# A ring for x, three key-feature buffers and a new opening order in a fused attention and rational-function kernel

## The chip, the cores and the metric

The kernel runs on one core of a Trainium2 chip. The metric is the time of one execution on the device in microseconds (us), as the median of several runs. Beside it stands one profiled execution, with every instruction of each engine: PE (TensorE matmuls), PEld (its weight loads), DVE (VectorE), ACT (ScalarE), POOL (GpSimd) and SP (SyncE, which here only issues DMAs).

## What is computed

There are 4 batches, 4 heads, 1088 positions and head dimension 32; the sketches have 8 rows, the second part has d_model = 128 and d_ff = 2048, on 4 x 1088 = 4352 tokens.

```python
def phi(x):                                    # 8 x 8 = 64 features of each row
    a = einsum('rd,bhsd->bhsr', S1, x); b = einsum('rd,bhsd->bhsr', S2, x)
    return einsum('bhsi,bhsj->bhsij', a, b).reshape(*x.shape[:-1], 64)
q_p, k_p = phi(q), phi(k)
kv = einsum('bhsf,bhsd->bhfd', k_p, v); z = k_p.sum(axis=2)
attn = einsum('bhsf,bhfd->bhsd', q_p, kv) / (einsum('bhsf,bhf->bhs', q_p, z)[..., None] + 1e-6)
x = attn.transpose(0, 2, 1, 3).reshape(4352, 128)
h = x @ w_in
g = (a[0] + a[1]*h + a[2]*h*h + a[3]*h*h*h) / (1 + abs(b[0])*abs(h) + abs(b[1])*h*h + 1e-6)
out = g @ w_out
```

## The kernel before

**Two halves, one list.** The attention half makes x, transposed (feature by token), in the tile xT; the second half reads xT and writes the output. All of it is written as small steps, and the list ORDER at the top of the file says in which sequence they are emitted, as `name:index`. Each engine runs its own instructions in that sequence and waits for others only through data, so a step's place in the list fixes its place in the queue of every engine that it uses, SP's queue of DMAs too.

**Keys.** For each batch, `kt` transposes the keys on DVE, `ks` makes the two sketches on PE, `kc` copies the second sketch out of PSUM on ACT, `kf` multiplies the sketches into the 64 features on DVE (tile k_p), `kp` multiplies the features with v on PE, and `kk` copies the result (kvz) on ACT. The first batch is cut into three parts (2, 2 and 5 of the nine 128-row tiles) and four transposes, kt0 to kt3; its keys come in three DMAs, the columns of the first four tiles as one and the rest as two. Sketches of the first batch lie in the two large PSUM buffers (`wide`, tile h_ps), later ones in the four small banks (`bank`, tile att_ps); both kinds are handed out in turn. k_p has two buffers.

**Queries.** Each batch is cut into blocks, numbered through, 4 in the first batch and 3 in the others. `qt` transposes (DVE), `qs` sketches (PE), `qc` copies (ACT; from block 3 on through DRAM, with DMAs on SP), `qf` multiplies (DVE), `qp` multiplies with kvz (PE), `qd`, `qi`, `qx` divide (ACT or DVE, then DVE), `qb` transposes back (PE) and `qk` copies the block into xT (ACT).

**The second half** works on 17 units of up to 4096 columns (unit 0: 256 tokens; then 512 tokens each in two units; at the end two of 256 tokens). `h` is the hidden matmul of a quarter of the unit (PE, tile h_ps), `e` its copy to bf16 (ACT, tile hh), `u`, `w`, `y` build the denominator on DVE, `ln` and `ex` invert it on ACT (tile r), `pa` or `pd` is one polynomial term on ACT or DVE (tile p, chosen by P_ON_ACT), `s`, `m`, `x` multiply on DVE, `G` is the output matmul (PE) and `st` transposes the output (DVE) and stores it (SP). In `u0`, `s1` and so on the digit is the half of the unit.

**Opening.** `tn` emits idle matmuls, as many as TURNS says at that index, on a bank of their own; a turn with 0 only takes a bank. `lw`, `lx`, `lk`, `lq`, `lv` issue loads of w_out, w_in, keys, queries and v. `wo` scales one of six half-parts of w_out to bf16, on ACT where W_ENG is 1, else on DVE; indices 2y and 2y+1 are the halves for factor y. The single v buffer, the single key buffer and the single kT make their next loads and transposes wait for their last readers.

The lines that a sentence can't say:

```python
self.take = wide if first else bank                                   # Keys
k_p = self.k_p[part] = tmp.tile([128, 5, H, R, R], FP, name="k_p")    # pool of two
nc.scalar.copy(out=xT[:, c:c + self.n], in_=self.xp[:, :self.n])      # Queries.keep
rhs=xT[:, t0:t0 + tl]                                                 # hidden
```

Of the kernel before, what the change touches and what calls it, by code (L numbers as in the profile page):

```python
# [25 lines left out]
ks0:1 y0:0 h1:1 lk:2 kc1:1 ex1:0 lq:2 kf1:1 h3:1 e1:1 s1:0 kc0:1 h0:1 e3:1 kf0:1 pa0:0 m1:0 h2:1 qf:3 e0:1 x1:0 qp:3
qc:4 e2:1 kt0:2 h0:2 ln0:0 u1:1 kt1:2 h1:2 w1:1 e0:2 ex0:0 y1:1 ks0:2 h2:2 e1:2 s0:0 qd:3 ln0:1 h3:2 qi:3 m0:0 e2:2
lk:3 qx:3 kp1:1 x0:0 e3:2 ex0:1 u1:2 qb:3 lv:2 G0:0 pd0:1 qk:3 w1:2 ln1:1 G1:0 G2:0 qf:4 G3:0 kc0:2 kk:1 y1:2 ex1:1
G4:0 G5:0 kf0:2 qp:4 ln0:2 s0:1 qs:5 G0:1 qd:4 qc:5 qi:4 ex0:2 qt:7 G1:1 qx:4 m0:1 qb:4 ks1:2 qk:4 s1:1 pa1:1 h2:3
s0:2 kc1:2 m1:1 h3:3 e2:3 kf1:2 h1:3 e3:3 st:0 x1:1 ln1:2 qs:7 x0:1 h0:3 e1:3 kt1:3 m0:2 h2:4 e0:3 pd1:2 pa0:2 u1:3  # L30
h3:4 qt:9 w1:3 e2:4 G2:1 ex1:2 x0:2 h0:4 qf:5 e3:4 kp1:2 s1:2 pa0:3 y1:3 h1:4 qc:7 e0:4 m1:2 ln0:3 qp:5 kt0:3 e1:4
G3:1 x1:2 ex0:3 G4:1 m0:3 G5:1 u1:4 ks0:3 qd:5 ln1:3 qi:5 G0:2 w1:4 G1:2 pa1:3 qx:5 G2:2 y1:4 lv:3 qb:5 G3:2 qk:5
ex1:3 h0:5 m1:3 v0:3 kk:2 ln0:4 h2:5 s1:3 e0:5 qs:6 G4:2 qf:7 ex0:4 h1:5 x0:3 qt:8 qc:6 e2:5 s0:4 e1:5 h3:5 pd0:4
pa1:4 m0:4 h1:6 v1:3 e3:5 x0:4 G5:2 ln1:4 u1:5 h3:6 st:2 e1:6 w1:5 qp:7 ex1:4 x1:3 h0:6 e3:6 y1:5 qd:7 pa0:5 lq:3 G0:3
G2:3 qi:7 s1:4 h2:6 e0:6 m0:5 ln0:5 m1:4 qs:8 G3:3 e2:6 qf:6 G5:3 x1:4 ex0:5 G0:4 u1:6 G1:4 qc:8 ln1:5 qp:6 v0:5 qx:7
w1:6 qb:7 qd:6 G2:4 pa0:6 qi:6 G3:4 qx:6 y1:6 qb:6 qk:7 G4:4 qk:6 ex1:5 h3:7 m0:6 pa1:5 G5:4 qt:10 s1:5 h1:7 e3:7 st:4
h2:7 e1:7 m1:5 ln0:6 x0:5 h0:7 e2:7 x1:5 qs:9 e0:7 h3:8 qf:8 ex0:6 u1:7 h1:8 v0:6 qc:9 ln1:6 w1:7 ks1:3 s0:6 e1:8 G0:5
y1:7 kc1:3 qp:8 ex1:6 h2:8 pd1:6 kc0:3 e3:8 s1:6 ln0:7 h0:8 kf0:3 e2:8 m1:6 G2:5 ex0:7 G3:5 x0:6 G4:5 kf1:3 qd:8 e0:8
qs:10 G5:5 ln1:7 qi:8 u1:8 kp1:3 qx:8 pa0:7 w1:8 qb:8 G0:6 qf:9 qk:8 y1:8 qc:10 h3:9 ex1:7 s0:7 h2:9 e3:9 s1:7 ln0:8
h0:9 m0:7 e2:9 x1:6 G2:6 e0:9 h1:10 x0:7 ex0:8 pd1:7 h1:9 m1:7 pa0:8 s0:8 G3:6 e1:9 u1:9 G0:7 qt:11 ln1:8 qp:9 qt:12  # L40
# [29 lines left out]
def kernel(  # L70
# [161 lines left out]
    class Keys:  # L232
        def __init__(self, b, k_sb, v_sb, first=False):
            self.b, self.dst, self.k_sb, self.v_sb = b, kvz[b % 2], k_sb, v_sb
            self.take = wide if first else bank
# [16 lines left out]

        def sketches(self, part):
            t0, n = self.PARTS[part]
            ab = self.ab[part] = self.take()[:, 0:n * H * 2 * R].rearrange("p (t h s r) -> p t h s r", h=H, s=2, r=R)
            for t in range(t0, t0 + n):
                nc.tensor.matmul(ab[:, t - t0].rearrange("p h s r -> p (h s r)"),  # L257
                                 lhsT=self.kT[:, t * 128:(t + 1) * 128],
                                 rhs=S12.rearrange("p h s r -> p (h s r)"), start=True, stop=True)
# [5 lines left out]

        def features(self, part):
            n = self.PARTS[part][1]
            k_p = self.k_p[part] = tmp.tile([128, 5, H, R, R], FP, name="k_p")
            nc.vector.tensor_mul(
                out=k_p[:, 0:n].rearrange("p t h i j -> p (t h) i j"),  # L270
                in0=self.ab[part][:, :, :, 0, :].rearrange("p t h r -> p (t h) r")[:, :, :, None]
                    .broadcast_to([128, n * H, R, R]),
                in1=self.sk[part][:, 0:n].rearrange("p t h r -> p (t h) r")[:, :, None, :]
                    .broadcast_to([128, n * H, R, R]))
# [38 lines left out]
    class Queries:  # L313
# [74 lines left out]

        def keep(self):
            c = self.b * S + self.c0  # L390
            nc.scalar.copy(out=xT[:, c:c + self.n], in_=self.xp[:, :self.n])
# [50 lines left out]
    def hidden(i, part):  # L442
# [3 lines left out]
        for x in range(per // 4):  # L446
            f = f0 + part * (per // 4) + x
            nc.tensor.matmul(t[:, x * tl:(x + 1) * tl], lhsT=w_in_sb[:, f * 128:(f + 1) * 128],  # L448
                             rhs=xT[:, t0:t0 + tl], start=True, stop=True)
# [261 lines left out]
```

## Time and profile before

| what | value |
|---|---|
| median of 3 runs | 273.89 us (273.89 to 274.06) |
| the profiled execution | 274.08 us |
| its span, first to last instruction | 272.3 us |
| busy PE / DVE / ACT | 258.4 / 256.0 / 250.2 us |
| DVE busy from 0 to 30.72 us | 20.3 us |
| granted TensorE clock, mean | 0.999 |

A row of the timeline begins with its start and its duration in us, then engine, line, operation, `written tile<-read tiles`, shape and count; in brackets at the end is the idle time before it and what ended it. A duration includes an instruction's way through the pipeline, so the next one can start before it is over. A row of groups ends with the busy time, the mean of one in ns, and the engine's idle time ahead of the group. L12 is line 12 of the kernel.

### The profile page before, as it was taken

How to read it: one execution, taken by the hardware profiler on the slowest of the kernel's cores; microseconds unless marked ns; L12 is line 12 of the kernel's file. 1: busy time of each engine (PE TensorE's matmuls, PEld its weight loads, DVE VectorE, ACT ScalarE, POOL GpSimd, SP SyncE). 2: the span in 40 equal slices, each digit the busy share in tenths (PEclk: the TensorE clock that was granted, in tenths of full speed). 3: DMA queues.
4: the chain of work that ended last, by engine and by line, in shares of the span. 5: the costliest groups of instructions: out<-in, count | busy, mean ns of one | idle time of the engine just before them, and what ended most of it. 6: DMA issues, size and time to landing. Idle time of an engine off the chain costs nothing.

```text
span 272.3 us, 3730 instructions
## 1 busy us (share of the span) xinstructions
PE 258.4 (95%) x1398; PEld 146.2 (54%) x1398; DVE 256.0 (94%) x277; ACT 250.2 (92%) x224; POOL 2.9 (1%) x24
## 2 busy tenths in 40 slices
PE   7989999999999899999999999999999998999763
PEld 2778656963564354545454554434545356675552
DVE  2876999999999999999999999999999999999993
ACT  1467999998999999999999999999999999999990
...
DMA packets 30530, 19.55 MB, mean 72 GB/s; under 512 B 20400, under 2 KB 26672, under 8 KB 30512
## 3 DMA queue, kind: packets, MB, share of 16 engines
...
q10 hardware_dynamic: 1520, 0.38, 0.7%
...
q14 instruction: 7, 0.06, 0.1%
...
## 4 chain that ended last, share of the span: by engine, by line
PE 35%; ACT 28%; DVE 23%; issue 9%; DMA 2%; SPq 1%; DVEq 0%; ACTq 0%
PE h_ps L448 17%; PE att_ps L581 9%; ACT hh L454 8%; ACT ln L539 7%; ACT r L543 7%; DVE s L547 4%; ACT p L534 4%; DVE g L551 4%; PE att_ps L361 3%; DVE g L562 3%; DVE w L488 3%; DVE w L483 2%; DMA k_sb<-in_k_dram 2%; PE att_ps L298 1%; PE att_ps L257 1%
## 5 line engine op out<-in xcount | busy, mean ns | idle before, releaser
L448 PE MATMUL h_ps<-xT,w_in_sb 128*128 128x512 f32 (+1 forms) x320 | 126.2, 536 | 2.3 <-ACT hh L454 1.6
L448 PEld LDWEIGHTS h_ps<-xT,w_in_sb 128*128 128x128 f32 x320 | 58.3, 190 | 52.8 <-issue 35.0
L454 ACT CAST hh<-h_ps 128x1024 bf16<-128x1024 f32 x68 | 68.2, 1022 | 4.2 <-PE h_ps L448 3.7
L581 PEld LDWEIGHTS <-w_out 128*128 128x128 bf16 x460 | 44.6, 98 | 46.0 <-issue 15.1
L543 ACT ACTIVATE r<-ln 128x2048 bf16<-128x2048 f32 (+1 forms) x35 | 65.9, 1883 | 0.3
L539 ACT ACTIVATE ln<-w 128x2048 f32<-128x2048 bf16 (+1 forms) x35 | 65.9, 1882 | 0.3
L534 ACT ACTIVATE p<-hh,a_sb 128x2048 bf16<-128x2048 bf16 (+1 forms) x23 | 46.7, 2035 | 0.1
L547 DVE TENSOR_TENSOR s<-hh,r 128x2048 bf16<-128x2048 bf16 (+2 forms) x33 | 40.9, 1243 | 0.2
L488 DVE TENSOR_TENSOR w<-w,u 128x4096 bf16<-128x4096 bf16 (+2 forms) x22 | 39.5, 1798 | 0.1
L581 PE MATMUL att_ps<-g,w_out 128*128 128x512 bf16 (+1 forms) x160 | 34.8, 347 | 3.6 <-DVE g L562 3.6
L551 DVE TENSOR_TENSOR g<-hh,s 128x2048 bf16<-128x2048 bf16 (+1 forms) x30 | 35.2, 1175 | 0.0
L581 PE MATMUL att_ps<-r,w_out 128*128 128x512 bf16 (+1 forms) x160 | 35.0, 347 | 0.0
L562 DVE TENSOR_TENSOR g<-g,p 128x2048 bf16<-128x2048 bf16 (+1 forms) x30 | 34.9, 1175 | 0.0
L581 PE MATMUL att_ps<-s,w_out 128*128 128x512 bf16 (+1 forms) x140 | 29.8, 343 | 0.9 <-DVE s L547 0.9
L483 DVE TENSOR_SCALAR w<-u,b_abs 128x4096 bf16<-128x4096 bf16 (+2 forms) x22 | 23.9, 1092 | 0.1
L477 DVE TENSOR_SCALAR u<-hh 128x4096 uint16<-128x4096 uint16 (+2 forms) x22 | 21.2, 968 | 0.9 <-ACT hh L454 0.8
L361 PEld LDWEIGHTS att_ps<-kvz,q_pT 128*128 128x128 f32 x144 | 17.6, 191 | 4.9 <-ACT sk_sb L408 1.0
L361 PE MATMUL att_ps<-kvz,q_pT 128*128 128x66 f32 x144 | 18.0, 274 | 0.9 <-DVE q_pT L353 0.5
L298 PEld LDWEIGHTS att_ps<-v_sb,k_p 128*64 128x64 f32 (+1 forms) x288 | 8.8, 138 | 2.6 <-issue 1.8
L529 DVE TENSOR_SCALAR p<-hh,a_sb 128x2048 bf16<-128x2048 bf16 x12 | 9.6, 799 | 0.0
L298 PE MATMUL att_ps<-v_sb,k_p 128*64 128x64 f32 (+1 forms) x288 | 9.5, 224 | 0.0
L425 DVE TENSOR_TENSOR q_pT<-a_all,b_all 128x768 f32<-128x768 f32 (+1 forms) x10 | 9.0, 896 | 0.0
...
## 6 DMA issues: line engine op xcount, KB each, us to landing
...
```

The source lines that it names most:

```text
L361: nc.tensor.matmul(self.nd[:, o:o + 2 * KW], lhsT=self.q_p[:, c, x:x + 128], rhs=kvz[self.b % 2][:, c, :], start=True, stop=True)
L448: nc.tensor.matmul(t[:, x * tl:(x + 1) * tl], lhsT=w_in_sb[:, f * 128:(f + 1) * 128], rhs=xT[:, t0:t0 + tl], start=True, stop=True)
L454: nc.scalar.copy(out=live[i]["hh"][:, part * PW:(part + 1) * PW], in_=live[i]["h", part])
L483: nc.vector.tensor_scalar(out=t[:, c], in0=live[i]["u"][:, c], scalar1=ab1, scalar2=ab0, op0=AX.mult, op1=AX.add)
L488: nc.vector.tensor_mul(out=t[:, c], in0=t[:, c], in1=live[i]["u"][:, c])
L534: nc.scalar.activation(out=part_of(i, "p", h), in_=hh, func=ACT.Identity, scale=a3, bias=a2)
L539: nc.scalar.activation(out=t, in_=live[i]["w"][:, span(h)], func=ACT.Ln, bias=1.0 + 1e-6)
L543: nc.scalar.activation(out=part_of(i, "r", h), in_=live[i]["ln"], func=ACT.Exp, scale=-1.0)
L547: nc.vector.tensor_mul(out=part_of(i, "s", h), in0=hh, in1=part_of(i, "r", h))
L551: nc.vector.tensor_mul(out=part_of(i, "g", h), in0=hh, in1=part_of(i, "p" if horner(i, first(h)) else "s", h))
L562: nc.vector.tensor_mul(out=g, in0=g, in1=part_of(i, "s" if horner(i, first(h)) else "p", h))
L581: nc.tensor.matmul(outs[t0][:, :tl], lhsT=w_sb[y][:, f0 + x, :], rhs=part_of(i, key, h)[:, c:c + tl], start=done[0] == 0, stop=done[0] == ...
```

## The change

Five things are changed.

- k_p gets three buffers in place of two.
- xT holds 2048 tokens and is used as a ring: token t lies at `(t - 256) % 2048`. A block that crosses the ring's edge is copied in two pieces; this is so for one block (tokens 2176 to 2560, cut at 2304).
- Of the first keys' sketches only the third part still lies in a large PSUM buffer; the first two lie in small banks.
- The first keys' loads change queues: the columns of the first four tiles are now issued by ACT, the others of the same rows by SP. The third, small one stays on ACT.
- ORDER is new, with TURNS and W_ENG. The four first transposes run in the order kt0, kt1, kt2, kt3 instead of kt0, kt2, kt3, kt1. All idle matmuls, 12 + 2 + 1 + 2, stand ahead of the first sketch; before, 12 stood there and 2 after the sketches. All three key parts are sketched, multiplied and summed ahead of the second query block; the products of block 2 (`qp:2`) stand ahead of the first hidden matmul, the sketch of block 3 (`qs:3`) behind two or three of them. w_out's part 3 is made on DVE instead of ACT. On SP's queue both halves of w_in precede the second keys, and v precedes the queries. From about the 250th of the 727 steps on, only neighbours are swapped. (LX is read nowhere.)

```diff
-TURNS = (10, 2, 0, 0, 2, 0, 0, 0, 0)
+TURNS = (12, 2, 0, 0, 1, 2, 0, 0, 0)
 ORDER = """
-tn:4 tn:0 lw:1 kt0:0 lq:0 kt2:0 lw:0 kt3:0 lx:1 kt1:0 ks0:0 lk:1 qt:0 ks2:0 kc0:0 lx:0 kf0:0 ba:0 qt:1 tn:1 kc2:0 qs:0
-kf2:0 kp0:0 qc:0 ks1:0 qf:0 kc1:0 kf1:0 qs:1 wo:1 qt:3 kp1:0 qc:1 kp2:0 qf:1 qt:2 qs:3 wo:4 kk:0 lq:1 lv:1 wo:2 qp:0
-wo:0 qs:2 qd:0 wo:5 qi:0 qx:0 qc:2 qb:0 qf:2 qk:0 wo:3 qp:1 kt0:1 qc:3 h2:0 qd:1 qi:1 qx:1 qt:5 h3:0 e2:0 qt:4 kt1:1
+tn:0 lw:1 lq:0 kt0:0 lw:0 kt1:0 lx:1 tn:1 kt2:0 lx:0 tn:4 kt3:0 tn:5 lk:1 ks0:0 qt:0 qt:1 ks1:0 kc0:0 ks2:0 kf0:0
+kc1:0 kf1:0 qs:0 kc2:0 kf2:0 kp0:0 qc:0 kp1:0 ba:0 qf:0 kp2:0 wo:3 qs:1 kk:0 lv:1 qt:3 qp:0 qt:2 qc:1 wo:1 lq:1 qf:1
+qs:2 qd:0 qi:0 qc:2 qp:1 qx:0 qf:2 wo:0 qb:0 qp:2 qd:1 wo:4 qk:0 qi:1 h3:0 qx:1 qd:2 wo:5 wo:2 h2:0 e3:0 kt1:1 kt0:1
...
-W_ENG = (1, 1, 0, 1, 0, 1)
+W_ENG = (1, 1, 0, 0, 0, 1)
...
-    nc.sync.dma_start(out=k0.rearrange("p (m x) -> p m x", m=NM)[:, :, 0:4 * D],
+    nc.scalar.dma_start(out=k0.rearrange("p (m x) -> p m x", m=NM)[:, :, 0:4 * D],
...
-    nc.scalar.dma_start(out=k0[:, 0:km].rearrange("p (m x) -> p m x", m=NM - 1)[:, :, 4 * D:],
+    nc.sync.dma_start(out=k0[:, 0:km].rearrange("p (m x) -> p m x", m=NM - 1)[:, :, 4 * D:],
...
-    xT = big.tile([d_model, n_tok], FP, name="xT")
+    XR = 2048
+    xT = big.tile([d_model, XR], FP, name="xT")
+
+    def x_at(t):
+        return (t - n_tok % 512) % XR
...
-            self.take = wide if first else bank
...
-            ab = self.ab[part] = self.take()[:, 0:n * H * 2 * R].rearrange("p (t h s r) -> p t h s r", h=H, s=2, r=R)
+            ab = (wide if self.first and part == 2 else bank)()[:, 0:n * H * 2 * R]
+            ab = self.ab[part] = ab.rearrange("p (t h s r) -> p t h s r", h=H, s=2, r=R)
...
-            k_p = self.k_p[part] = tmp.tile([128, 5, H, R, R], FP, name="k_p")
+            k_p = self.k_p[part] = tmp.tile([128, 5, H, R, R], FP, name="k_p", bufs=3)
...
-            nc.scalar.copy(out=xT[:, c:c + self.n], in_=self.xp[:, :self.n])
+            cut = min(self.n, XR - x_at(c))
+            for x, y in ((0, cut), (cut, self.n)):
+                if x < y:
+                    nc.scalar.copy(out=xT[:, x_at(c + x):x_at(c + x) + y - x], in_=self.xp[:, x:y])
...
-                             rhs=xT[:, t0:t0 + tl], start=True, stop=True)
+                             rhs=xT[:, x_at(t0):x_at(t0) + tl], start=True, stop=True)
```

More of the change, by code (lines that the diff above doesn't have):

```diff
@@ L26 @@
[L26 to L40, printed above, removed]
@@ new lines @@
+ln1:0 h2:1 w0:0 qt:6 y0:0 kc1:1 ex1:0 h0:1 kf1:1 e2:1 ks0:1 s1:0 e0:1 h1:1 m1:0 kc0:1 pa0:0 kf0:1 h3:1 lq:2 kt0:2 e1:1
+x1:0 e3:1 h0:2 ln0:0 u1:1 h2:2 qf:3 w1:1 qc:4 e0:2 qp:3 e2:2 kt1:2 y1:1 ex0:0 h1:2 s0:0 h3:2 ln1:1 m0:0 kp1:1 e3:2
+x0:0 qd:3 e1:2 qi:3 pd0:1 ex1:1 G0:0 qx:3 lv:2 u1:2 G1:0 ln0:1 G2:0 w1:2 lk:3 G3:0 y1:2 qs:5 kk:1 ex0:1 qb:3 G4:0
+ks0:2 qk:3 qf:4 G5:0 kc0:2 ln0:2 kf0:2 qp:4 s0:1 qc:5 G0:1 qd:4 ex0:2 qi:4 qx:4 G1:1 s1:1 qb:4 ks1:2 qk:4 s0:2 pa1:1
+h2:3 kt1:3 m0:1 kc1:2 h3:3 qt:7 e2:3 m1:1 kf1:2 h0:3 e3:3 ln1:2 x1:1 qs:7 h1:3 x0:1 e0:3 st:0 m0:2 h2:4 e1:3 pd1:2
@@ new lines @@
+pa0:2 h3:4 u1:3 qf:5 e2:4 kp1:2 w1:3 qc:7 ex1:2 x0:2 h0:4 e3:4 s1:2 pa0:3 qt:9 qp:5 y1:3 e0:4 h1:4 qd:5 m1:2 ln0:3
+G2:1 qi:5 x1:2 G3:1 e1:4 kt0:3 lv:3 G4:1 ex0:3 u1:4 ks0:3 G5:1 m0:3 pa1:3 G0:2 w1:4 G1:2 ln1:3 qx:5 G2:2 y1:4 qb:5
+G3:2 qk:5 ex1:3 h0:5 m1:3 kk:2 v0:3 ln0:4 h2:5 s1:3 G4:2 e0:5 ex0:4 qf:7 h1:5 x0:3 e2:5 qs:6 s0:4 qc:6 e1:5 h3:5 pd0:4
+pa1:4 m0:4 h1:6 v1:3 x0:4 e3:5 G5:2 e1:6 u1:5 qp:7 ln1:4 qt:8 st:2 h3:6 w1:5 ex1:4 x1:3 G0:3 e3:6 h0:6 y1:5 pa0:5 lq:3
+G2:3 s1:4 h2:6 e0:6 m0:5 qd:7 ln0:5 G3:3 qi:7 m1:4 G5:3 e2:6 qf:6 qs:8 ex0:5 x1:4 G0:4 G1:4 u1:6 qc:8 ln1:5 qp:6 v0:5
@@ new lines @@
+qx:7 w1:6 qb:7 qd:6 pa0:6 G2:4 qi:6 G3:4 qx:6 y1:6 qb:6 qk:7 G4:4 qk:6 ex1:5 h3:7 m0:6 pa1:5 G5:4 s1:5 h1:7 e3:7 qt:10
+h2:7 st:4 e1:7 m1:5 ln0:6 h0:7 x0:5 e2:7 x1:5 e0:7 h3:8 qf:8 ex0:6 u1:7 qs:9 v0:6 h1:8 qc:9 ln1:6 w1:7 ks1:3 s0:6 e1:8
+G0:5 y1:7 kc1:3 ex1:6 qp:8 h2:8 pd1:6 kc0:3 e3:8 s1:6 ln0:7 h0:8 kf0:3 e2:8 m1:6 G2:5 ex0:7 x0:6 G3:5 G4:5 kf1:3 qd:8
+e0:8 qs:10 G5:5 ln1:7 qi:8 u1:8 kp1:3 qx:8 pa0:7 w1:8 qf:9 qb:8 G0:6 qk:8 y1:8 qc:10 ex1:7 h3:9 s0:7 h2:9 e3:9 s1:7
+ln0:8 h0:9 m0:7 e2:9 x1:6 G2:6 e0:9 h1:10 x0:7 ex0:8 pd1:7 h1:9 m1:7 pa0:8 s0:8 G3:6 e1:9 u1:9 G0:7 qt:11 ln1:8 qp:9
@@ new lines @@
+qt:12 u0:9 m0:8 h3:10 e1:10 w1:9 qd:9 ex1:8 qf:10 h2:10 x0:8 e3:10 x1:7 G4:6 kk:3 e2:10 h0:10 y1:9 pa0:9 w0:9 qp:10
+qi:9 y0:9 e0:10 G1:7 qx:9 qd:10 ln0:9 qi:10 s1:8 qb:9 G5:6 u1:10 G2:7 qk:9 ex0:9 G3:7 qx:10 m1:8 qb:10 G4:7 qk:10
+pd1:8 ln1:9 qs:11 s0:9 h1:11 qc:11 w1:10 ex1:9 h0:11 m0:9 e1:11 x1:8 G5:7 e0:11 h3:11 y1:10 pa1:9 G0:8 s1:9 e3:11
+h2:11 ln0:10 x0:9 h0:12 m1:9 e2:11 pd0:10 ex0:10 h1:12 u1:11 x1:9 G1:8 ln1:10 G2:8 w1:11 G3:8 e0:12 s0:10 G0:9 e1:12
+y1:11 G4:8 ex1:10 G5:8 G1:9 m0:10 ln0:11 G2:9 qf:11 h2:12 s1:10 ex0:11 x0:10 h3:12 pa1:10 m1:10 qs:12 s0:11 G3:9 qc:12
@@ new lines @@
+e2:12 G4:9 pd0:11 ln1:11 G5:9 m0:11 qp:11 x1:10 e3:12 G0:10 x0:11 qd:11 ex1:11 G1:10 qi:11 u1:12 G2:10 pa1:11 qx:11
+G3:10 w1:12 qb:11 G4:10 qk:11 s1:11 pa0:12 h1:13 y1:12 h3:13 e1:13 m1:11 ln0:12 h2:13 st:6 x1:11 ex0:12 G5:10 qf:12
+G0:11 st:10 e3:13 qp:12 s0:12 e2:13 st:8 h0:13 ln1:12 m0:12 u1:13 h2:14 e0:13 x0:12 ex1:12 u0:13 h3:14 w1:13 e2:14
+w0:13 y1:13 e3:14 h1:14 qd:12 pa1:12 y0:13 h0:14 s1:12 e1:14 qi:12 m1:12 G1:11 e0:14 G2:11 qx:12 ln1:13 u1:14 G3:11
+x1:12 qb:12 G4:11 ex1:13 w1:14 G5:11 G0:12 qk:12 pd0:13 ln0:13 h0:15 y1:14 ex0:13 h2:15 pd1:13 s1:13 e0:15 G1:12 s0:13
@@ new lines @@
+ln0:14 G2:12 h3:15 m1:13 e2:15 m0:13 ex0:14 h1:15 x1:13 x0:13 e3:15 G3:12 e1:15 G4:12 s0:14 ln1:14 G0:13 u1:15 G5:12
+m0:14 h2:16 pa0:14 w1:15 h3:16 ex1:14 st:12 y1:15 G1:13 e2:16 e3:16 h1:16 x0:14 ln0:15 u2:16 u3:16 h0:16 w2:16 s1:14
+ex0:15 w3:16 G2:13 y2:16 pd0:15 e1:16 G0:15 y3:16 e0:16 G3:13 s0:15 pa1:14 u0:16 G1:15 m0:15 G4:13 ln1:15 w0:16 G5:13
+m1:14 G0:14 ex1:15 y0:16 G1:14 G2:14 v1:14 ln0:16 G3:14 pd1:15 s1:15 ex0:16 x0:15 x1:14 G2:15 ln2:16 m1:15 G5:14
+ex2:16 s0:16 G0:16 pa0:16 x1:15 G3:15 st:14 ln3:16 m0:16 G4:15 ex3:16 s2:16 G1:16 x0:16 pa2:16 G5:15 m2:16 pa3:16
@@ L57 @@
+G2:16 s3:16 G3:16 x2:16 G4:16 st:15 G5:16 m3:16 G6:16 G7:16 x3:16 G8:16 st:16
 """.split()
-W_ENG = (1, 1, 0, 1, 0, 1)
+W_ENG = (1, 1, 0, 0, 0, 1)
 P_ON_ACT = (1, 1, 0, 1, 1, 0, 1, 1, 0, 1, 1, 1, 1, 0, 1, 0, 1, 0, 1, 1, 0, 1, 0, 1, 1, 1, 0, 0, 1, 1, 0, 0, 1, 1)
@@ L61 @@
 QUARTER = (16,)
-LX = 2
+LX = 4
 TAIL = 2
```

18 lines of the change are left out of this document (1 added, 17 removed).

## The prediction

> **What bounds the kernel now.** I read the busy time in three stretches first, then who waited for whom after the opening, then the opening instruction by instruction. The stretches (columns: span, then busy us and count of PE, weight loads, DVE, ACT, POOL, granted clock, DMA share, GB/s):
>
> ```profile
> 0.00:30.72 30.72, 28.10 (x219) 20.47 (x220) 20.30 (x41) 18.12 (x30) 2.92 (x24) 1.00 0.80 221
> 30.72:264.00 233.28, 226.64 (x1151) 122.90 (x1150) 232.09 (x231) 231.02 (x195) 0.00 (x0) 1.00 0.21 52
> 264.00:272.30 8.30, 3.64 (x32) 2.84 (x30) 3.63 (x7) 1.04 (x1) 0.00 (x0) 0.97 0.43 64
> ```
>
> From 30.72 to 264 us DVE is idle 233.28 - 232.09 = 1.19 us and ACT 2.26 us. Two engines are full there, so the end is fixed by when that stretch begins, by the work in it, and by the few waits left. The waits from 30 to 262 us (total, times, longest) are these:
>
> ```profile
> DVE u L477 <- ACT hh L454: 0.6, 2, 0.3
> ACT hh L454 <- PE h_ps L448: 1.1, 2, 0.7
> ```
>
> In the first 30.72 us DVE is idle 10.42 us. That is the only large store of time, and the new order works there. From roughly the 250th step on, the two orders differ in swaps of neighbours only. So I work out when DVE and ACT reach the same point of their work (the end of the second y of unit 0, at 30.72 us before) and carry that difference to the end.
>
> **The opening on TensorE, step by step.** First the weight loads of two idle matmuls and the start of the twelfth, then TensorE's whole opening (start, duration, what it waited for):
>
> ```profile
> 5.00 0.15 PEld L170 LDWEIGHTS <-idle 128*128 128x128 bf16 x1 [0.28 <-issue]
> 5.43 0.15 PEld L170 LDWEIGHTS <-idle 128*128 128x128 bf16 x1 [0.28 <-issue]
> 5.70 0.38 PE L170 MATMUL att_ps<-idle 128*128 128x512 bf16 x1
> ```
>
> ```profile
> 1.19 4.89 PE L170 MATMUL att_ps<-idle 128*128 128x512 bf16 x12 [1.19 <-DVE idle L165]
> 6.51 2.05 PE L257 MATMUL h_ps<-S,kT 128*128 128x64 f32 x14 [0.43 <-DVE kT L251]
> 8.39 0.59 PE L170 MATMUL att_ps<-idle 128*128 128x512 bf16 x2
> 8.92 1.13 PE L334 MATMUL h_ps<-qT,SAB 64*128 64x256 f32 x8
> 9.98 0.69 PE L298 MATMUL att_ps<-v_sb,k_p 128*64 128x64 f32 x16
> 10.60 0.66 PE L257 MATMUL h_ps<-S,kT 128*128 128x64 f32 x4
> 11.46 1.13 PE L334 MATMUL h_ps<-qT,SAB 64*128 64x256 f32 x8 [0.21 <-DVE q_pT L350]
> 12.53 1.85 PE L298 MATMUL att_ps<-v_sb,k_p 128*64 128x64 f32 x56
> 14.21 0.44 PE L402 MATMUL att_ps<-qT,S 128*64 128x160 f32 x4
> 14.87 1.11 PE L361 MATMUL att_ps<-kvz,q_pT 128*128 128x66 f32 x8 [0.22 <-ACT kvz L308]
> 15.91 1.13 PE L334 MATMUL att_ps<-qT,SAB 64*128 64x256 f32 x8
> 17.02 0.41 PE L387 MATMUL att_ps<-ident,x_tok 128*128 128x128 f32 x2
> 17.96 1.11 PE L361 MATMUL att_ps<-kvz,q_pT 128*128 128x66 f32 x8 [0.52 <-DVE q_pT L353]
> 18.90 0.43 PE L448 MATMUL h_ps<-xT,w_in_sb 128*128 128x256 f32 x1
> ```
>
> *Idle matmuls.* Before, 12 stand ahead of the first sketch and 2 after it; now 12 + 2 + 1 + 2 = 17 stand ahead and none after. The spacing is 5.43 - 5.00 = 0.43 us while the array is slow and 8.39's two take 0.59 - 0.38 = 0.21 us when it is fast; the twelfth starts 0.27 us after its load, so the change falls near 5.6 us. Twelve are issued by 5.91, five more at 0.21 end at 7.0. The first sketch, which waited for kT until 6.51, now waits for them: +0.5.
>
> *Key sketches.* The three parts follow each other on the three transposes, now in the same order as TensorE wants them. Before, 14 passes went from 6.51 to 8.39 with one stop of some 0.2 for a transpose, so 0.12 each; 18 are 2.15: 9.15. Then the first query sketch, 9.98 - 8.92 = 1.06: 10.2, against 9.98 before.
>
> *Key products.* Before, 16 passes at 9.98, a stop for one part's late sketch, then 56 at 12.53. Now all parts are sketched, and 72 passes run through if the features come: 0.62 + (14.21 - 12.53) = 2.3: 12.5. The features of the long part set this:
>
> ```profile
> 8.59 0.29 ACT L264 COPY b_sk<-h_ps 128x160 f32<-128x160 f32 x1 [0.24 <-PE h_ps L257]
> ...
> 8.92 1.49 DVE L269 TENSOR_TENSOR k_p<-h_ps,b_sk 128x1280 f32<-128x1280 f32 x1 [0.17 <-ACT b_sk L264]
> ```
>
> The copy starts 0.2 after the sketches' issue: 9.3 to 9.6; the product runs 9.6 to 11.1. TensorE reaches it after the first two parts at 10.2 + 0.62 + 0.5 = 11.3, so it is covered by 0.2. This is what the third buffer does: with two, this third product would wait until the first part's matmuls ended (10.8), 1.2 us later. The own banks for the first two parts keep the third's sketch from waiting for their features in the same way. The ring itself only makes room; its reads are over a ring's length old, so I give its waits nothing, and its one wrapped copy at most one more 0.39 of ACT (row at 17.61 below).
>
> *Queries.* Second query sketch 12.53 - 11.46 = 1.07: 13.55. Block 0's products 15.91 - 14.87 = 1.04: 14.6. Block 2's sketch 17.02 - 15.91 = 1.11: 15.7. Block 1's products 18.90 - 17.96 = 0.94: 16.65. The transposes back 0.41: 17.05. Block 2's products, which ran after the first hidden matmuls, 0.94: **18.0**, where the first hidden matmul starts, against 18.90. The gaps of 0.22 and 0.52 before 14.87 and 17.96 go because the kv copies and block 1's features are early. That is -0.9 in spite of one block more and five idle matmuls.
>
> *The other feeds.*
>
> ```profile
> 17.07 0.65 ACT L344 COPY a_all<-att_ps 128x256 f32<-128x256 f32 x2
> 17.61 0.39 ACT L391 COPY xT<-att_ps 128x256 f32<-128x256 f32 x1
> 17.87 1.17 ACT L616 ACTIVATE w_out<-w_out_sb_f,a_sb 128x1024 bf16<-128x1024 f32 x1
> ...
> 22.61 1.01 ACT L454 CAST hh<-h_ps 128x1024 bf16<-128x1024 f32 x1 [0.71 <-PE h_ps L448]
> 23.65 2.10 ACT L534 ACTIVATE p<-hh,a_sb 128x2048 bf16<-128x2048 bf16 x1
> ...
> 28.39 1.94 ACT L539 ACTIVATE ln<-w 128x2048 f32<-128x2048 bf16 x1
> ```
>
> The copy at 17.07 follows its sketch by 1.16, so now 15.75 to 16.4; one w_out part (1.17) and x (0.39) follow: x at 18.0, level with TensorE. One w_out part goes from ACT (1.17) to DVE:
>
> ```profile
> L618 DVE TENSOR_SCALAR w_out<-w_out_sb_f,a_sb 128x1024 bf16<-128x1024 f32 x1 | 0.7, 744 | 0.0
> ```
>
> On DVE its 0.74 stands where DVE next waits for the second query sketch (till 13.6), from 11.7 to 12.4, so it is hidden there; uncovered it costs 0.74.
>
> *To the full stretch.* From the hidden matmuls on, the second evacuation keeps its distance of 22.61 - 18.90 = 3.71: 21.7. ACT's p follows 1.04 later, at 22.75. On DVE the second u and y of unit 0 close the opening:
>
> ```profile
> 22.09 1.04 DVE L321 STREAM_TRANSPOSE qT<-q_sb 128x384 f32<-128x384 f32 x2 [2.13 <-DMA q_sb<-in_q_dram]
> ...
> 28.00 0.69 DVE L477 TENSOR_SCALAR u<-hh 128x2048 uint16<-128x2048 uint16 x1
> ...
> 29.58 1.23 DVE L488 TENSOR_TENSOR w<-w,u 128x2048 bf16<-128x2048 bf16 x1
> ```
>
> ACT then has p, a sketch copy, two evacuations and two x copies as before (the last 23.65 to 28.39), so ln starts at 27.5, -0.9. The two x copies end there, so the last evacuation ends at about 26.95, and DVE's second u starts; u, w, one transpose and y take 3.1 (28.00 to 30.72 before, and 0.4 for the transpose): 30.05, **-0.7** against 30.72, with the w_out part already done.
>
> Further on, DVE gets one wait more and loses one:
>
> ```profile
> L547 DVE TENSOR_TENSOR s<-hh,r 128x2048 bf16<-128x2048 bf16 x29 | 35.0, 1212 | 0.2
> ```
>
> Unit 1's u needs its four evacuations: ACT has ln 1.94, r about the same, p 2.10, four evacuations of 1.01 and small copies of 0.6 ahead, less 0.1 of overlap each: 27.5 + 9.8 = 37.3. DVE comes there from 30.05 with two key features (1.49, 1.2), s, m and x (1.21 each) and a transpose (1.07), less overlap: 36.9. The query features, which filled this before, now stand behind. So 0.4 is lost; 0.2 of wait ahead of an s goes, and ACT is 0.2 further ahead than DVE and gives the rest back. -0.7 stands. Of the later waits for evacuations (0.6), some go: ACT sheds 1.17 and up to 1.1 of waits, less 0.39, while DVE gains 0.74 of work. Between 0 and -0.6 I take -0.2, nearer to none, since each order makes waits of its own. The last 8.3 us keep their chain (last products, transpose, stores).
>
> *Loads.* The two large first key loads change queues. The first part's wait ends with kT just before 6.51; a later or earlier arrival of up to 0.5 is hidden by the idle matmuls, which end at 7.0. So I give the exchange itself nothing.
>
> **Sum.** 274.08 (the profiled execution: span 272.3 and 1.78 around it) - 0.7 - 0.2 = 273.2. That execution lies 0.19 above the median of 273.89, so 273.0 by the median. What the measurement can tell from no change is about 0.2%, 0.55 us: faster means under 273.3, slower over 274.4.
>
> **Rivals.**
> *Idle matmuls stay slow (slower).* For it: all 17 precede the first sketch, and from 1.19 to 18.0 TensorE has no gap left that could absorb them. If the array stays at 0.43 for all, they end at 1.19 + 17 x 0.43 = 8.5, 1.5 later; then -0.9 becomes +0.6: 274.5. It decides once more than four of the five extra run slow. Against it: the change to fast came at the twelfth here, and the start is the same. [...]
>
> *The saving is used up by new waits (no change).* Two full engines with 1.19 and 2.26 us of idle have no room; a few swaps that each open 0.2 leave -0.3: 273.6. One place with a price is batch 1's queries, which landed at 22.09 before: v's four loads now stand ahead of them in SP's queue. They are needed at 25.7; each us that they come after that pushes the second u by as much, less 0.3 that DVE waits there anyway.
>
> *The later waits vanish wholly, TensorE's lead included.* -0.7 - 0.6 - 0.3 = -1.6: 272.3. For it: ACT is 1.2 us lighter. Against: DVE is heavier by 0.74 and as full.
>
> *The third buffer does nothing* would be so if the features were not ready before the first products end; then the opening is 1.2 us longer, and -0.9 becomes +0.3, 274.2. The sketches' times above speak against it.
>
> **How the numbers follow.** Forecast 0.45 (273.0; 0.10 of it comes to lie within 0.2%), later waits gone 0.15, saving used up 0.22, idle matmuls slow 0.12, buffer idle 0.06. Faster: 0.35 + 0.15 + 0.05 of the third case = 0.55. Slower: 0.12 + 0.03 of the buffer's case = 0.15. Same: the rest, 0.30. The range reaches from the case of vanished waits, 272.2, to the slow idle matmuls, 274.5.
>
> **What would show it.** In the profile after: 17 idle matmuls ending near 7.0 and the first sketch there; one unbroken run of 72 product passes ending near 12.5; the first hidden matmul near 18.0; ln near 27.5 and y's end near 30.05 with DVE idle about 9 us till then; DVE idle from there to the end of the full stretch about 1 us. I am wrong if the first sketch comes after 7.5, if the products wait for the long features, or if DVE loses more than 1.5 us after 30 us.

## The result, and the profile after

| | before | after |
|---|---|---|
| median of 22 runs each, us | 273.90 (273.57 to 274.94) | 273.25 (272.58 to 274.55) |
| ratio, 95% interval | | 0.9979 (0.9972 to 0.9986) |
| profiled execution, us | 274.08 | 272.58 |
| its span, us | 272.3 | 270.8 |

The change saves 0.65 us by the medians, about what was forecast (0.9). The profiled execution of after is the fastest of its 22 runs, so the profile shows more than the median does: 1.5 us. Keep that apart in all that follows. The runs after lie 1.97 us apart, those before 1.37.

The three stretches of after (span; busy us and count of PE, weight loads, DVE, ACT, POOL; clock; DMA share; GB/s), cut where DVE has ended the second y of unit 0:

```profile
0.00:29.07 29.07, 27.88 (x216) 20.47 (x217) 20.61 (x42) 17.06 (x29) 2.92 (x24) 1.00 0.74 212
29.07:262.40 233.33, 226.22 (x1154) 123.16 (x1153) 232.40 (x231) 230.82 (x196) 0.00 (x0) 1.00 0.23 56
262.40:270.80 8.40, 3.87 (x32) 3.02 (x31) 3.84 (x7) 1.19 (x2) 0.00 (x0) 0.99 0.23 34
```

The opening is 29.07 us against 30.72, and DVE's idle time in it 29.07 - 20.61 = 8.46 against 10.42. The full stretch is as long as it was (233.33 against 233.28): 0.26 us less of DVE's idle time, 0.31 more of its work. So the whole gain was made in the opening. TensorE there (start, duration, what it did):

```profile
1.19 5.45 PE L170 MATMUL att_ps<-idle 128*128 128x512 bf16 x17 [1.19 <-DVE idle L165]
6.47 1.00 PE L261 MATMUL att_ps<-S,kT 128*128 128x64 f32 x8
...
8.52 1.13 PE L338 MATMUL h_ps<-qT,SAB 64*128 64x256 f32 x8
9.63 2.32 PE L302 MATMUL att_ps<-v_sb,k_p 128*64 128x64 f32 x72
11.88 1.13 PE L338 MATMUL h_ps<-qT,SAB 64*128 64x256 f32 x8
...
17.15 2.21 PE L455 MATMUL h_ps<-xT,w_in_sb 128*128 128x256 f32 x9
```

One unbroken run of 72 product passes, and the first hidden matmul at 17.15 (18.90 before). Why this execution is ahead even of the forecast stands in the weight loads of the idle matmuls:

```profile
3.72 0.15 PEld L170 LDWEIGHTS <-idle 128*128 128x128 bf16 x1 [0.28 <-issue]
4.15 0.15 PEld L170 LDWEIGHTS <-idle 128*128 128x128 bf16 x1 [0.28 <-issue]
4.53 1.61 PEld L170 LDWEIGHTS <-idle 128*128 128x128 bf16 x8 [0.23 <-issue]
6.26 1.08 PEld L261 LDWEIGHTS att_ps<-S,kT 128*128 128x128 f32 x8
```

Up to 4.15 they come 0.43 apart, then eight come in 1.61. In the kernel before, the wide spacing still held at 5.43. So the array turned fast earlier in this execution (its matmuls then started 0.21 us apart, at 4.75, 4.96 and 5.18, about half the 0.43), and the idle matmuls made way at 6.26, not at 7.0. The clock column says 1.00 for the whole opening: it does not show this.

On DVE (first key transpose; second keys; first u; the end of the second y; what follows it):

```profile
4.76 1.66 DVE L254 STREAM_TRANSPOSE kT<-k_sb 128x256 f32<-128x256 f32 x4 [1.14 <-DMA k_sb<-in_k_dram]
...
20.39 1.37 DVE L254 STREAM_TRANSPOSE kT<-k_sb 128x224 f32<-128x224 f32 x2 [2.19 <-DMA k_sb<-in_k_dram]
21.68 0.16 DVE L380 RECIPROCAL rec<-den 128x8 f32<-128x8 f32 x1
21.95 0.69 DVE L484 TENSOR_SCALAR u<-hh 128x2048 uint16<-128x2048 uint16 x1
...
27.97 1.18 DVE L495 TENSOR_TENSOR w<-w,u 128x2048 bf16<-128x2048 bf16 x1
29.07 1.48 DVE L273 TENSOR_TENSOR k_p<-att_ps,b_sk 128x1280 f32<-128x1280 f32 x1
```

The second keys now land at 20.4, about as late as DVE can bear: their transposes end just before the first u.

### The profile page after: what moved, and what is told of

Same layout as the page of the kernel before. It is cut to its first block, busy times and chain, and to the rows that moved or that the text cites. A ratio compares the mean times of both kernels' runs of the same rounds, so it can differ in the third digit from the quotient of the medians.

```text
span 270.8 us, 3744 instructions
## 1 busy us (share of the span) xinstructions
PE 258.0 (95%) x1401; PEld 146.6 (54%) x1401; DVE 256.8 (95%) x278; ACT 249.1 (92%) x224; POOL 2.9 (1%) x24
## 3 DMA queue, kind: packets, MB, share of 16 engines
HBM read 16.16 MB, written 3.15 MB: 71 GB/s over the span
## 4 chain that ended last, share of the span: by engine, by line
ACT 38%; DVE 27%; PE 25%; issue 8%; DVEq 0%; ACTq 0%
ACT hh L461 11%; ACT ln L546 10%; PE h_ps L455 9%; ACT r L550 9%; ACT p L541 7%; PE att_ps L588 7%; DVE g L558 5%; DVE g L569 5%; DVE s L554 4%; DVE w L495 4%; DVE w L490 3%; PE att_ps L365 2%; PE att_ps L170 2%; PE att_ps L302 2%; DVE u L484 2%
## 5 line engine op out<-in xcount | busy, mean ns | idle before, releaser
L273 DVE TENSOR_TENSOR k_p<-att_ps,b_sk 128x1280 f32<-128x1280 f32 (+2 forms) x8 | 9.4, 1178 | 0.0
```

## The experiments

**The theory** after the result: only the opening counts; the new order shortens it, and the third buffer and the small banks are what lets the order run without a stop. **Its rivals:** the exchanged loads bring the gain (the first transposes start 1.25 us earlier in the profile after), or the w_out part moved off ACT does. Each ratio below is to runs of the kernel before taken beside it, whose medians lie between 273.92 and 274.23.

One table serves all. It has, from each profile, the start of the first key transpose, of the first sketch's weight load, of the first hidden matmul, and of the key features behind the second y (all in us), then the span and the difference of the last two:

| kernel | kT | sketch | hidden | behind y | span | rest |
|---|---|---|---|---|---|---|
| before | 6.01 | 6.51 | 18.90 | 30.72 | 272.3 | 241.6 |
| after | 4.76 | 6.26 | 17.15 | 29.07 | 270.8 | 241.7 |
| e9, after again | 5.24 | 6.31 | 17.41 | 29.84 | 271.3 | 241.5 |
| e1, loads as before | 6.13 | 7.59 | 18.44 | 30.36 | 272.0 | 241.6 |
| e8, w_out part on ACT | 5.18 | 7.42 | 18.27 | 30.20 | 272.1 | 241.9 |
| e3, two buffers | 5.39 | 7.18 | 19.48 | 31.41 | 273.1 | 241.7 |
| e7, no small banks | 5.19 | 7.31 | 18.96 | 30.88 | 272.7 | 241.8 |
| e4, old order | 5.04 | 5.53 | 18.68 | 30.50 | 272.2 | 241.7 |
| e2, before with new loads | 5.19 | 5.69 | 18.77 | 30.59 | 272.2 | 241.6 |
| e6, 24 idle matmuls | 5.08 | 7.72 | 18.57 | 30.50 | 272.4 | 241.9 |
| e5, 12 idle matmuls | 4.89 | 5.39 | 17.20 | 29.13 | 270.8 | 241.7 |
| e10, none | 5.08 | 5.58 | 19.87 | 31.80 | 273.7 | 241.9 |
| e11, 12 and v on two queues | 5.16 | 5.66 | 17.14 | 29.06 | 270.8 | 241.7 |
| e12, 12 and keys earlier | 5.15 | 5.85 | 17.50 | 30.04 | 271.8 | 241.8 |

The last column moves by 0.4 us while the opening moves by 2.7. The span of every one of these executions is its opening plus 241.7, within 0.2.

### The order alone, and without its buffers

e4: the changed kernel with the old lists; three buffers, the ring, the small banks and the new loads stay.

```diff
-TURNS = (12, 2, 0, 0, 1, 2, 0, 0, 0)
+TURNS = (10, 2, 0, 0, 2, 0, 0, 0, 0)
...
-tn:0 lw:1 lq:0 kt0:0 lw:0 kt1:0 lx:1 tn:1 kt2:0 lx:0 tn:4 kt3:0 tn:5 lk:1 ks0:0 qt:0 qt:1 ks1:0 kc0:0 ks2:0 kf0:0
+tn:4 tn:0 lw:1 kt0:0 lq:0 kt2:0 lw:0 kt3:0 lx:1 kt1:0 ks0:0 lk:1 qt:0 ks2:0 kc0:0 lx:0 kf0:0 ba:0 qt:1 tn:1 kc2:0 qs:0
...
-W_ENG = (1, 1, 0, 0, 0, 1)
+W_ENG = (1, 1, 0, 1, 0, 1)
```

> The changed kernel with the order, the idle matmuls and the w_out engines of the kernel before; the ring, three buffers, own banks and exchanged loads stay. Theory (the order carries the gain): 273.5 to 273.9, with the first hidden matmul after 18.2 us. Rival (the parts carry it): 273.25 and the first hidden matmul near 17.2.

Measured: 274.02 us (273.35 to 274.84), ratio 1.0003 (0.9993 to 1.0012). Buffers, ring, banks and loads bring nothing without the order. The ring was not taken out of the changed kernel alone, so what it does there beside making room stays open.

e3: the changed kernel with two buffers for k_p.

```diff
-            k_p = self.k_p[part] = tmp.tile([128, 5, H, R, R], FP, name="k_p", bufs=3)
+            k_p = self.k_p[part] = tmp.tile([128, 5, H, R, R], FP, name="k_p")
```

> The changed kernel with two buffers for key features. Theory (from the prediction): the third product waits until the first part's matmuls end, so it starts at about 10.3 us instead of 8.95, the second query sketch at about 13.2 instead of 11.9, and the time is 0.8 to 1.3 us above 273.25. Rival: the wait is covered by the first two parts' matmuls, and the time is 273.25.

Measured: 274.43 us (273.84 to 274.89), ratio 1.0015 (1.0006 to 1.0023), so 0.36% above the changed kernel's 0.9979, some 1.0 us. TensorE and DVE of e3:

```profile
10.56 1.15 PE L302 MATMUL att_ps<-v_sb,k_p 128*64 128x64 f32 x32
12.89 1.39 PE L302 MATMUL att_ps<-v_sb,k_p 128*64 128x64 f32 x40 [1.19 <-DVE k_p L273]
```

```profile
8.26 1.26 DVE L273 TENSOR_TENSOR k_p<-att_ps,b_sk 128x512 f32<-128x512 f32 x2
11.35 1.49 DVE L273 TENSOR_TENSOR k_p<-h_ps,b_sk 128x1280 f32<-128x1280 f32 x1 [1.84 <-PE att_ps L302]
```

Read the two together: DVE waits 1.84 us for the first part's products to give a buffer back, then TensorE waits 1.19 for DVE. That is the 1.2 that the prediction put on the missing buffer. From sketch to first hidden matmul e3 takes 12.30 us (19.48 - 7.18) against 10.89 in after; the broken run of passes costs the other 0.2.

e7: all sketches of the first keys in the two large buffers.

```diff
-            ab = (wide if self.first and part == 2 else bank)()[:, 0:n * H * 2 * R]
+            ab = (wide if self.first else bank)()[:, 0:n * H * 2 * R]
```

> The changed kernel with all first key sketches in the two large PSUM buffers again. Theory: the third sketch waits for the first part's features, about 8.0 us instead of 7.3, and the time is 0.4 to 0.7 us above 273.25. Rival: the long features are late for another reason and the time is 273.25.

Measured: 274.34 us (273.89 to 275.77), ratio 1.0010 (0.9998 to 1.0022), 0.31% or 0.85 us above the changed kernel. TensorE of e7:

```profile
7.53 1.00 PE L261 MATMUL h_ps<-S,kT 128*128 128x64 f32 x8
9.11 1.33 PE L261 MATMUL h_ps<-S,kT 128*128 128x64 f32 x10 [0.58 <-DVE k_p L273]
```

The third part's sketches wait for the first part's features to give back a large buffer. So with either half of the room missing, all that the order gains is lost, with two buffers more than that: the order is worth something only with both.

### The loads and the w_out part

e1: the changed kernel with the first two key loads on their old queues. e2: the kernel before with them on the new ones.

```diff
-    nc.scalar.dma_start(out=k0.rearrange("p (m x) -> p m x", m=NM)[:, :, 0:4 * D],
+    nc.sync.dma_start(out=k0.rearrange("p (m x) -> p m x", m=NM)[:, :, 0:4 * D],
...
-    nc.sync.dma_start(out=k0[:, 0:km].rearrange("p (m x) -> p m x", m=NM - 1)[:, :, 4 * D:],
+    nc.scalar.dma_start(out=k0[:, 0:km].rearrange("p (m x) -> p m x", m=NM - 1)[:, :, 4 * D:],
```

> The changed kernel with the first two key loads on their old queues (first four tiles on SP, the rest on ACT). Theory A (the exchange made the keys come early): the first key transpose starts at about 6.0 us as in the kernel before, not at 4.8, the third key sketch starts about 0.3 later than 7.3, the first hidden matmul at about 17.4, and the time is 0.2 to 0.4 us above the changed kernel's 273.25. Theory B (the arrival differs from run to run, the queue does not matter): the transpose starts at 4.8 here too, and the time is 273.25.

> The kernel before with only the two loads exchanged. Theory A: first key transpose at about 4.8 us; the first hidden matmul moves from 18.9 to about 18.4, since the old order has other waits behind the sketches, and the time is 0.2 to 0.5 us under 273.9. Theory B: transpose at about 6.0 and the time 273.9.

Measured: e1 273.32 us (272.95 to 273.86), ratio 0.9973 (0.9963 to 0.9983); e2 274.04 us (273.57 to 274.56), ratio 0.9999 (0.9990 to 1.0007). Taking the exchange back costs nothing, adding it brings nothing. So theory A had the arrival right and its cost wrong. The exchange does something all the same. The first transpose in e1, and where e2 loses the time again:

```profile
6.13 1.49 DVE L254 STREAM_TRANSPOSE kT<-k_sb 128x256 f32<-128x256 f32 x4 [2.18 <-DMA k_sb<-in_k_dram]
```

```profile
5.69 0.66 PE L257 MATMUL h_ps<-S,kT 128*128 128x64 f32 x4
...
10.09 0.69 PE L298 MATMUL att_ps<-v_sb,k_p 128*64 128x64 f32 x16 [0.41 <-DMA v_sb<-in_v_dram]
```

With the old queues the first transposes start at 6.01 and 6.13 us, with the new ones at 4.76 to 5.39 in all twelve profiles. In e2 the sketches do start 0.8 us earlier, and the products then wait for v. In the changed kernel the 17 idle matmuls are still running when the keys are there.

e8: the w_out part back on ACT.

```diff
-W_ENG = (1, 1, 0, 0, 0, 1)
+W_ENG = (1, 1, 0, 1, 0, 1)
```

> The changed kernel with w_out part 3 on ACT as before. Theory: ACT waits 1.5 us for the key products at that place and DVE waits there too, so the part is hidden on either engine and the time is within 0.2 us of 273.25. Rival (total work of the full engines decides): DVE has 0.74 us less to do, and the time is 0.5 to 0.7 us lower; or ACT decides, and it is up to 1.1 us higher.

Measured: 273.47 us (272.58 to 273.96), ratio 0.9970 (0.9958 to 0.9982). No difference: DVE or ACT, the part is hidden in the opening.

### The idle matmuls

e5 keeps 12 of the 17, e6 has 24, e10 none; e9 is the changed kernel again, beside e10.

```diff
-TURNS = (12, 2, 0, 0, 1, 2, 0, 0, 0)
+TURNS = (12, 0, 0, 0, 0, 0, 0, 0, 0)    # e5
+TURNS = (12, 4, 0, 0, 4, 4, 0, 0, 0)    # e6
+TURNS = (0, 0, 0, 0, 0, 0, 0, 0, 0)     # e10
```

> The changed kernel with 12 idle matmuls ahead of the sketches instead of 17. Theory (idle matmuls stand in the way of the keys): the first sketch starts 0.8 to 1.1 us earlier, at 5.3 to 5.7, the first hidden matmul at about 16.4, and the time is 0.5 to 0.9 us under 273.25. Rival (they pay by making the array fast): the array stays slow in the sketches, the first hidden matmul comes no earlier than 17.1, and the time is 273.25 or more, with as wide a spread.

> The changed kernel with 24 idle matmuls ahead of the sketches. Theory: seven more at 0.21 us put the first sketch at 7.8 us and the first hidden matmul at about 18.6, and the time is 1.2 to 1.5 us above 273.25. Rival (the sketches wait for something else): less than 0.4 above.

> The changed kernel itself again, beside the next two. Theory A (the opening's length is carried to the end one for one, and with 17 idle matmuls it hangs on the moment at which the array turns fast): ratio to before 0.998 as at first, its single runs spread over about 1.5 us, and in the profile the end of the second y of unit 0 lies 241.7 us ahead of the span's end wherever the array turned fast (29.1 if at 4.5 us, 30.4 if at 7.1 us). Theory B (the spread comes from later waits): the distance from that y to the end differs from 241.7 by 0.5 us or more.

> No idle matmuls at all. Theory A: the first sketch starts as its keys come, at 5.4 us, but on a slow array: 18 sketch passes of 0.12 us become 0.25 or more, the array turns fast only some 3.5 us after that start, and the query sketch and the first products wait; first hidden matmul at 18 to 19 us, so the time is that of before within 0.3% and above the kernel with 12 idle matmuls by 0.8 to 1.8 us. Rival C (the idle matmuls are useless altogether, the loads bound the opening): products at 9.7 us with v's landing as with 12, first hidden matmul at 17.2, ratio 0.9957.

| idle matmuls | us (lowest to highest) | ratio to before (95%) |
|---|---|---|
| 0 (e10) | 276.12 (275.56 to 276.34) | 1.0073 (1.0059 to 1.0086) |
| 12 (e5) | 273.00 (272.65 to 273.12) | 0.9957 (0.9945 to 0.9969) |
| 17 (after) | 273.25 (272.58 to 274.55) | 0.9979 (0.9972 to 0.9986) |
| 17 (e9) | 273.08 (272.91 to 273.92) | 0.9972 (0.9960 to 0.9984) |
| 24 (e6) | 274.74 (273.96 to 275.35) | 1.0016 (1.0004 to 1.0028) |

With 24 the sketches are free at 7.72 us though the array turned as early as in after, and the time is that of before or worse: here the idle matmuls stand in the way. With 12 the ratio lies below that of after and its interval apart from it; from e9's, which has fewer runs, the interval is not apart. In plain microseconds e5 is only 0.08 and 0.25 below those two, since the runs of before beside it were the longest of all (274.23). So that 17 are also too many is likely, not shown. TensorE of e5:

```profile
1.19 4.05 PE L170 MATMUL att_ps<-idle 128*128 128x512 bf16 x12 [1.19 <-DVE idle L165]
5.39 1.10 PE L261 MATMUL att_ps<-S,kT 128*128 128x64 f32 x8 [0.15 <-DVE kT L254]
...
9.68 2.32 PE L302 MATMUL att_ps<-v_sb,k_p 128*64 128x64 f32 x72 [0.70 <-DMA v_sb<-in_v_dram]
```

Now the sketches wait for the keys and the products for v. So the first hidden matmul comes at 17.20, not at the expected 16.4. In its profile e5 is no faster than the profile of after (270.8 us both): after had the early array. What e5 gains, as far as one can tell, is that this matters less, since the keys and v set its times: its runs, only five, lie within 0.47 us. None at all is far worse; e10:

```profile
5.58 1.97 PE L261 MATMUL att_ps<-S,kT 128*128 128x64 f32 x8 [5.58 <-DVE kT L254]
7.34 2.34 PE L261 MATMUL h_ps<-S,kT 128*128 128x64 f32 x10
9.62 2.08 PE L338 MATMUL h_ps<-qT,SAB 64*128 64x256 f32 x8
11.62 3.04 PE L302 MATMUL att_ps<-v_sb,k_p 128*64 128x64 f32 x72
```

The first eight sketches take 1.97 us where after needs 1.00, the query sketch 2.08 for 1.13, and the 72 products 3.04 for 2.32, so part of them is slow too. Expected was a loss of 0.8 to 1.8 us against e5; it is 1.0073 - 0.9957, some 3.2 us. The direction of theory A held, its size did not: the array stayed slow for at least some 6 us from its first matmul (5.58 to 11.6). Theory A's 3.5 was the author's estimate, and no run shows it as a fixed time: with idle matmuls the last load at the wide spacing came 2.5 to 5.9 us behind the first matmul (3.72 to 7.13, from 1.19). Why it took so long here is open.

How far the array's turn moves shows in the last weight load of an idle matmul that came 0.43 us behind the one before it: 3.72 us in e5, 4.15 in after and e6, 4.57 in e2, e4 and e9, 5.00 in e11, 6.3 in e3 and e7, 6.71 in e8 and 7.13 in e1 (in before the load of the twelfth, at 5.43, still came 0.43 behind, and only that matmul was fast; in e12 all twelve in front were slow). Of e1:

```profile
6.28 0.15 PEld L170 LDWEIGHTS <-idle 128*128 128x128 bf16 x1 [0.28 <-issue]
6.71 0.15 PEld L170 LDWEIGHTS <-idle 128*128 128x128 bf16 x1 [0.28 <-issue]
7.13 0.34 PEld L170 LDWEIGHTS <-idle 128*128 128x128 bf16 x2 [0.28 <-issue]
7.59 0.52 PEld L261 LDWEIGHTS att_ps<-S,kT 128*128 128x128 f32 x3
```

With the same 17 in front, the first sketch is free at 6.26 in after and at 7.59 here, and e9, the same kernel as after, lies with after. Nothing in e1's edit touches the idle matmuls. Over all these profiles the turn moves by 7.13 - 3.72 = 3.41 us, read in steps of the wide spacing, 0.43; what sets its moment is not shown.

After and e9, the only two profiles of one kernel, turn just one step apart. That the turn also parts the runs of one kernel can be read, though not shown outright, from the mean clock of each run. In after, e1, e8 and e9, the 21 runs with a mean of 0.990 or less took 273.28 to 273.96 us, and of the 23 with 0.998 or more all but two took 272.58 to 273.25. The low mean comes from a late dip (0.96 from 220 to 262 us in e1, e6 and e8). The dip itself costs nothing that shows: with it 241.6 (e1) and 241.9 (e6, e8) lie behind y, without it 241.5 to 241.9 (e9, e10), and in e6 the runs with 0.992 or less are the short ones (up to 274.63; the others from 274.73). So it only marks a group of runs, and each profile fits its group: e1 and e8 have the dip and turn late, after and e9 have none and turn early, and e6 has the dip and turns early. Why the dip and the turn go together is open.

e9 was to show whether later waits make runs differ (its rival, B). In this execution they do not: its last column is 241.5. But its opening ends at 29.84, where theory A had 29.1 for so early a turn, as it has a second source. DVE of e9:

```profile
21.69 1.37 DVE L254 STREAM_TRANSPOSE kT<-k_sb 128x224 f32<-128x224 f32 x2 [3.23 <-DMA k_sb<-in_k_dram]
22.98 0.16 DVE L380 RECIPROCAL rec<-den 128x8 f32<-128x8 f32 x1
23.07 0.64 DVE L484 TENSOR_SCALAR u<-hh 128x2048 uint16<-128x2048 uint16 x1
```

The second keys landed 1.3 us later than in after and pushed the first u to 23.07, though ACT had done its input by 22.2 (21.17 and 1.01). From the first hidden matmul to the end of y it takes 12.43 us here and 11.92 or 11.93 in after, e1, e3, e5, e6, e7, e8, e10 and e11.

### Two attempts at more

e11: 12 idle matmuls, and two of the four first v loads issued by ACT ahead of its table load.

```diff
-            nc.sync.dma_start(out=t[m * 32:(m + 1) * 32, :, 0:w], in_=vv[:, :, m * W:m * W + w])
+            (nc.scalar if b == 0 and m > 1 else nc.sync).dma_start(out=t[m * 32:(m + 1) * 32, :, 0:w],
+                                                                   in_=vv[:, :, m * W:m * W + w])
...
-    nc.scalar.preload_act_table_set("natural_log_exp_and_others")
     load_v(0)
+    nc.scalar.preload_act_table_set("natural_log_exp_and_others")
```

> 12 idle matmuls, and two of the four loads of the first values issued from ACT's queue ahead of its table load, so that SP issues only two. Theory A: with 12 the key products waited 0.70 us for the values at 9.68; now they start at 9.0 behind the query sketch, the long part's 40 passes wait for the third feature until 10.1 and end at 11.4 instead of 11.93, the first hidden matmul comes at 16.7, and all is carried to the end: 0.3 to 0.6 us below the kernel with 12, ratio to before 0.994. Rival D (the transfers share the same engines, so another queue brings nothing): the values land at 9.6 again and the ratio is 0.996 as with 12.

Measured: 272.73 us (272.61 to 272.83), ratio 0.9955 (0.9942 to 0.9969). ACT's queue of DMA issues (ACTq) and its table load in e11:

```profile
3.58 2.66 ACTq L132 DMA_DIRECT2D v_sb<-in_v_dram  x2
6.26 1.28 ACT L160 ACT_TABLE_LOAD   x1 [6.26 <-DMA k_sb<-in_k_dram]
```

SP's queue in e11, then in e5:

```profile
2.86 2.62 SPq L132 DMA_DIRECT2D v_sb<-in_v_dram  x2
```

```profile
2.85 3.15 SPq L132 DMA_DIRECT2D v_sb<-in_v_dram  x4
```

TensorE of e11:

```profile
5.82 1.00 PE L262 MATMUL att_ps<-S,kT 128*128 128x64 f32 x8
...
9.48 2.46 PE L303 MATMUL att_ps<-v_sb,k_p 128*64 128x64 f32 x72 [0.27 <-DMA v_sb<-in_v_dram]
```

The two issues took 2.66 us on ACT, and the two left on SP took 2.62. So the last of v's loads was issued by 6.24, later than with all four on SP in e5 (6.00), and v landed at 9.48 against 9.68; with all four on SP it varies as much (9.97 in e12). So rival D was nearer in the outcome: the split hardly moves the arrival. Whether shared transfers are the reason is not shown, as the issue itself did not end sooner. Its ratio is the lowest of all, but cannot be told from e5's; both are below the changed kernel, e11 by 0.35 us against e9 beside it.

e12: 12 idle matmuls, and the second keys loaded ahead of the second half of w_in, as before the change.

```diff
-tn:0 lw:1 lq:0 kt0:0 lw:0 kt1:0 lx:1 tn:1 kt2:0 lx:0 tn:4 kt3:0 tn:5 lk:1 ks0:0 qt:0 qt:1 ks1:0 kc0:0 ks2:0 kf0:0
+tn:0 lw:1 lq:0 kt0:0 lw:0 kt1:0 lx:1 tn:1 kt2:0 tn:4 kt3:0 tn:5 lk:1 lx:0 ks0:0 qt:0 qt:1 ks1:0 kc0:0 ks2:0 kf0:0
```

> 12 idle matmuls, and batch 1's keys loaded ahead of the second half of w_in (as in the kernel before) instead of behind it. Theory A (the keys' late landing is the second thing that makes runs differ: they landed between 20.4 and 21.7 us, and from about 20.45 on their two transposes of 1.37 us push the first u): the keys land about 1.5 us earlier, DVE's wait ahead of their transposes falls from 2.2 us to under 1, the first u starts 0.03 us behind the fourth evacuation as it did at best, and the end of the second y stays at 29.1; ratio 0.9953 to 0.9957, single runs no wider apart than 0.5 us. Rival E (the second half of w_in is then the late one): the hidden matmuls pause for it, the second y ends 0.5 us or more later, and the ratio is 0.998 or above.

Measured: 273.66 us (273.02 to 274.09), ratio 0.9982 (0.9970 to 0.9993). DVE and TensorE of e12:

```profile
18.87 1.37 DVE L254 STREAM_TRANSPOSE kT<-k_sb 128x224 f32<-128x224 f32 x2 [0.32 <-DMA k_sb<-in_k_dram]
...
27.05 0.69 DVE L484 TENSOR_SCALAR u<-hh 128x2048 uint16<-128x2048 uint16 x1 [0.80 <-ACT hh L461]
```

```profile
21.65 1.97 PE L455 MATMUL h_ps<-xT,w_in_sb 128*128 128x256 f32 x8 [0.44 <-DMA w_in_sb<-in_moe_w_in_dram]
```

Rival E was right. The keys come 1.5 us earlier, as theory A had it, but the hidden matmuls then stop for w_in, and the second u waits 0.80 us. (Another 0.3 us of e12's late y is not the edit's: its products waited for v until 9.97, in e5 until 9.68.) The change's place for the keys is the better one; both loads are due within a microsecond of each other (20.4 for the keys, 21.2 for w_in).

## Why the prediction was right

**Two full engines, so carry the opening's difference to the end:** right, and the firmest finding: 241.5 to 241.9 us remain in fourteen profiles.

**Idle matmuls end at 7.0:** as one number this was the weakest step. The kernels with 17 gave 6.26, 6.31, 7.18, 7.31, 7.42 and 7.59. The prediction read one moment, 5.6 us, off one execution and held it fixed ("the start is the same"); it moves by 3.4 us between executions (3.72 to 7.13). Its rival, all 17 slow, never came in full (8.5), but the array turned later than forecast in four of the six. That 7.0 is close to the mean of the six (7.01) was luck: the one execution that was read turned near the middle of the range. The moving turn is also why the profile shows 1.5 us of gain and the median 0.65, as far as the groups of runs above can tell: e1 and e8, whose ratios are those of after, show the late end, with 273.86 and 273.88 us in their profiled executions.

**Sketch to first hidden matmul, 7.0 to 18.0:** 11.0 forecast, 10.89 in after and 10.85 in e1, e6 and e8. The unbroken 72 passes, forecast at 2.3, took 2.32. **The third buffer, 1.2 us, and the small banks:** right, as e3 and e7 show; with two buffers 274.2 was forecast and 274.43 measured.

**First hidden matmul to the end of y, 12.05 forecast:** 11.92. ln came 9.31 us behind the first hidden matmul (26.46 - 17.15; forecast 9.5). Missed here was the second keys' load. The prediction named v ahead of the queries as the risk on SP's queue; those caused no wait (q at 24.87 stands right behind y). It did not price both halves of w_in ahead of the second keys: 0 in after, 0.5 in e9.

**The exchange of loads at nothing:** right by e1 and e2, but not because arrivals stay within 0.5: they came 0.6 to 1.4 us earlier. The idle matmuls hid more than was said. In e1's profile the array turned late, so what the later keys would cost after an early turn is not shown.

**The w_out part hidden on DVE:** right by e8. It ran from 11.25, not 11.7.

**Later waits -0.2:** not seen. The two rows of DVE's waits from 30 to 262 us that are left:

```profile
DVE s L554 <- ACT r L550: 0.3, 1, 0.3
DVE rec L380 <- ACT den L376: 0.2, 1, 0.2
```

0.5 against 0.8 before, but the same stretch holds 0.31 us more of DVE's work, so the rest of the run grew by 0.15 (241.73 against 241.58); in e9, the same kernel, it is 0.12 shorter than before (241.46), so neither sign stands. And the wait of 0.4 at unit 1's u is not there: DVE came at 36.17 (its x from 34.99 for 1.18), ACT's fourth evacuation ended at 36.19. By the forecast's sum, -0.7 and -0.2 make -0.9; the medians say -0.65, to which the opening's -0.7 alone comes nearer.
